# Forgetting attention and two feed-forward layers on one core: the first pair's scores without placement, and every other matmul on the whole array

## The chip, the core and the metric

One core of a Trainium2 chip runs the whole program. The metric is the device time of one execution in microseconds (us), from the first to the last instruction with what lies around it; lower is better. A core has five engines with queues of their own: TensorE (PE, with its weight loads as PEld), VectorE (DVE), ScalarE (ACT), GpSimd (POOL) and SyncE (SP), which here sends nearly all transfers. The transfers are carried out by 16 DMA engines.

## What is computed

An attention with 4 batches, 8 heads, 576 positions and 64 numbers per head, whose scores get a decay from a running sum of logarithms, and then two feed-forward layers on 2304 tokens of 512 numbers:

```python
scores = scale * np.matmul(q, k.transpose(0, 1, 3, 2))
log_f = np.log(np.clip(f, 0.0001, 1.0))
cum = np.cumsum(log_f, axis=-1)
decay = cum[:, :, :, None] - cum[:, :, None, :]
scores = np.where(causal, -1000000000.0, scores + decay)
attn = np.exp(scores - np.max(scores, axis=-1, keepdims=True))
attn = attn / (np.sum(attn, axis=-1, keepdims=True) + 1e-09)
x = np.matmul(attn, v)            # then laid out as 2304 x 512
h = x @ w_in;  x = (h - np.tanh(h)) @ w_out
h = x @ w_in2; out = (h / (1.0 + np.exp(-h))) @ w_out2
```

## The kernel before

**Precision.** Most matmuls run on numbers marked F32R, and the kernel splits each number into a rounded part hi and a rest lo and multiplies hi·hi, hi·lo and lo·hi. A matmul on plain float32 shows in the trace as two weight loads and two matmuls. The odd head's values (L548, L549) are of that second kind.

**Tiles.** Attention runs over 16 pairs of heads. A pair has nine tiles: four row blocks of 128 queries of the even head (i = 0 to 3, with 128 to 512 keys), a tile with the last 64 queries of both heads together (`h` = 2, `i` = 4), and four of the odd head. Tile n passes through `scores` two steps ahead, `least` (DVE, mask and minimum), `expo` (ACT, exponential and row sum), `guard` and `normalise` (DVE adds 1e-9 and takes the reciprocal of two tiles' sums, POOL multiplies), and after LAG = 9 steps `transposes` (PE), `evac_a` and `evac_b` (ACT, DVE) and `values` (PE). The order is written out by hand in the loop at L682; each engine works through its own queue in that order.

**Scores.** A score tile takes two matmuls. For them q and k, hi and lo, and the decay rows are placed by DMA (`place`, L394) into `kqa` (128 rows: hi over lo) and `kqb` (68 rows: the third product over four decay rows). There are two such buffers, for even and odd pairs. A pair's placement is ten transfers between places in SBUF and one of decay rows from DRAM, all on SP's queue. `split` (L378) makes hi and lo from the loaded `kqraw`, on POOL and DVE (in pair 0 also ACT). Pair 1's hi and lo lie in `pth` and `ptl`, which hold the transposed probabilities later; all others lie in one pair of buffers `kqhi`, `kqlo`.

**Decay rows.** `decay_rows` (L87) fills constants on POOL, clips f and scans its logarithm, and DVE and ACT write four rows per head into pair 1's still unused `kqa` and `kqb`. Two transfers take them to DRAM, from where each pair's placement reads its own.

**Values.** For the even head, `values` (L539) multiplies `vals` (hi and lo of v side by side, 128 columns) by `pth` and `ptl`. For the odd head it uses the 64 columns of `vraw` of that head and plain float32. Keys 512 to 575 are chunk c = 4, with 64 rows. The transposes of that chunk (L518) have 64 columns. `collect_a` and `collect_b` copy the outcome into x, and the odd head's goes from partitions 0 to 63 to 64 to 127.

**Feed-forward.** `hidden` (L252) and `project` (L311) run matmuls of 512 columns from the end of the attention on; `wload` and `wdecode` load and decode the weights, of which the first four chunks are loaded during the attention.

Of the kernel before, what the change touches and what calls it, by code (L numbers as in the profile page):

```python
# [7 lines left out]
F32 = mybir.dt.float32  # L8
# [18 lines left out]
NPT = 448 * 4 + S  # L27

# [9 lines left out]
def forgetting_attention_two_ffn(  # L38
# [25 lines left out]
    def setup_consts(const):  # L64
        ident = const.tile([P, P], F32, name="ident")
        nc.gpsimd.memset(ident, 0.0)
        nc.gpsimd.affine_select(
            out=ident, in_=ident, pattern=[[-1, P]], compare_op=ALU.not_equal,
            fill=1.0, base=0, channel_multiplier=1,
        )  # L70
# [5 lines left out]
        )  # L76
        mask4 = const.tile([P, S // 2], F32, name="mask4")
# [7 lines left out]
        return ident, mask, mask4  # L85

    def decay_rows(pool, ft, room):  # L87


        BH = B * H  # L90
        rows = [a[:, j, :] for a in room for j in range(2)]
        kc, q0, q1 = slice(K0, Q0), slice(Q0, Z1), slice(Q1, W)
        for r, a in enumerate(rows):
            nc.gpsimd.memset(rd(a[:, Z1:Q1]), 0.0)
            nc.gpsimd.memset(rd(a[:, 0:K0]), 0.0)
            for c in ((kc,) if r % 2 else (q0, q1)):
                nc.gpsimd.memset(rd(a[:, c]), 1.0 / SCALE)
        ones = pool.tile([P, S], F32, tag="p", name="ones")[0:BH]
        nc.vector.memset(ones, 1.0)
        nc.vector.tensor_scalar(ft, ft, 1e-4, 1.0, ALU.max, ALU.min)  # L100
        lf = pool.tile([P, S], F32, tag="p", name="lf")[0:BH]
        nc.scalar.activation(lf, ft, AF.Ln)
        cum = pool.tile([P, S], F32, tag="p", name="cum")[0:BH]
        nc.vector.tensor_tensor_scan(cum, ones, lf, 0.0, ALU.mult, ALU.add)
        nc.scalar.mul(rows[0][:, kc], cum, -1.0)
        nc.vector.tensor_copy(rows[1][:, q0], cum[:, 0:512])
        nc.vector.tensor_copy(rows[1][:, q1], cum[:, 512:S])
        nc.vector.tensor_tensor(rows[3][:, q0], cum[:, 0:512], rd(rows[1][:, q0]), ALU.subtract)
        nc.vector.tensor_tensor(rows[3][:, q1], cum[:, 512:S], rd(rows[1][:, q1]), ALU.subtract)
        nc.vector.scalar_tensor_tensor(  # L110
            rows[2][:, kc], cum, -1.0, rd(rows[0][:, kc]), ALU.mult, ALU.subtract
        )
        dec = dram.tile([4, BH, W], F32, name="dec")
        for i, a in enumerate(room):
            nc.sync.dma_start(out=dec[2 * i:2 * i + 2].rearrange("r p w -> p r w"), in_=rd(a))
        return dec
# [639 lines left out]
```

## Time and profile before

| | us |
|---|---|
| median of three runs | 1046.52 |
| lowest, highest | 1042.13, 1047.77 |
| the profiled execution | 1043.61 |
| its span, first to last instruction | 1041.5 |
| PE busy in it | 1001.6 (96%) |
| DVE, ACT, POOL busy | 612.3, 491.3, 199.8 |

The busy times are sums over stages with different limits: POOL works in the attention alone. In the traces, L12 is line 12 of the kernel, `out_t<-ptf,vraw 128*64 128x512` names the tile written and those read, the rows and columns of the array that the weights take, and the shape of what streams through. "x2" stands for two equal instructions one behind the other, given with the first one's start and the time from there to the last one's end.

### The profile page before, as it was taken

Reading aid. Unit: us, or ns where it says so; the run is one execution under the profiler, and the core shown is the slowest. Engines: PE = TensorE matmul, PEld = TensorE weight load, DVE = VectorE, ACT = ScalarE, POOL = GpSimd, SP = SyncE. Lnnn points to the kernel's source line nnn. Section 1 sums busy time; section 2 is a strip of 40 time slices with the busy share of each in tenths; the row PEclk is TensorE's granted clock in tenths of the full one; section 3 lists DMA queues with packets and bytes.
Section 4 is the critical chain, followed back from the end, with each engine's and each line's share of the span. In section 5 each row is a group of like instructions: output and inputs, shape, how many; then the busy total and the mean of one; then the engine's idle time right before and its main releaser. Section 6 shows DMA issues by size and latency. Waiting matters only on the chain.

```text
span 1041.5 us, 14028 instructions
## 1 busy us (share of the span) xinstructions
PE 1001.6 (96%) x4912; PEld 812.2 (78%) x4912; DVE 612.3 (59%) x1430; ACT 491.3 (47%) x1089; POOL 199.8 (19%) x293
## 2 busy tenths in 40 slices
PE   2599999999999999999999999999999999999998
PEld 2467666665888888898888988888888888888887
DVE  4479888988766646565556875334443555533323
ACT  3477778786545443343333543433443444332322
POOL 6578878887100000000000000000000000000000
PEclk9899999999999999999999999999999999999999
DMA  8988898742221201111102211101001111001111
GB/s 217 270 224 224 233 233 229 202 124 81 81 69 54 81 1 41 41 41 41 41 2 80 81 42 41 36 6 61 25 38 41 41 41 41 1 0 41 41 41 61
DMA packets 29621, 85.65 MB, mean 82 GB/s; under 512 B 4496, under 2 KB 4496, under 8 KB 29488
## 3 DMA queue, kind: packets, MB, share of 16 engines
q1 hardware_dynamic: 29552, 84.76, 28.1%
q8 instruction: 39, 0.64, 0.3%
q14 instruction: 30, 0.25, 0.1%
HBM read 49.49 MB, written 5.37 MB: 53 GB/s over the span
## 4 chain that ended last, share of the span: by engine, by line
PE 90%; DMA 4%; SPq 2%; DVE 2%; POOL 1%; issue 1%; ACT 1%; DVEq 0%; POOLq 0%
PE a L311 38%; PE h L252 38%; PE out_t L553 6%; PE t L507 4%; SPq L373 2%; DMA kqb<-kqhi 2%; PE s L431 1%; PE s L430 1%; DMA kqa<-pth 1%; PE misc L443 1%; PE s L443 1%; DMA kqa<-kqhi 1%; PE misc L553 1%; DMA kqa<-ptl 0%; DMA kqa<-kqlo 0%
## 5 line engine op out<-in xcount | busy, mean ns | idle before, releaser
L252 PE MATMUL h<-xh,wh 128*128 128x512 f32 (+1 forms) x640 | 236.3, 369 | 0.0
L252 PE MATMUL h<-xl,wh 128*128 128x512 f32 (+1 forms) x640 | 235.6, 368 | 0.0
L252 PE MATMUL h<-xh,wl 128*128 128x512 f32 (+1 forms) x640 | 235.4, 368 | 0.0
L274 DVE TENSOR_TENSOR gl<-g,gh 128x512 fp32r<-128x512 f32 (+1 forms) x158 | 101.4, 642 | 101.7 <-ACT gh L270 99.8
L252 PEld LDWEIGHTS h<-xh,wh 128*128 128x128 f32 x640 | 120.7, 189 | 23.3 <-issue 2.8
L270 ACT CAST gh<-g 128x512 fp32r<-128x512 f32 (+1 forms) x160 | 92.6, 579 | 95.0 <-DVE g L267 92.5
L252 PEld LDWEIGHTS h<-xl,wh 128*128 128x128 f32 x640 | 120.7, 189 | 20.2
L252 PEld LDWEIGHTS h<-xh,wl 128*128 128x128 f32 x640 | 120.5, 188 | 20.0
L311 PE MATMUL a<-gh,wh 128*128 128x512 f32 (+1 forms) x320 | 117.9, 368 | 0.0
L311 PE MATMUL a<-gl,wh 128*128 128x512 f32 (+1 forms) x320 | 117.8, 368 | 0.0
L311 PE MATMUL a<-gh,wl 128*128 128x512 f32 (+1 forms) x320 | 117.7, 368 | 0.0
L311 PE MATMUL a<-wh,gh 128*128 128x512 f32 x288 | 112.2, 390 | 0.0
L311 PE MATMUL a<-wl,gh 128*128 128x512 f32 x288 | 112.2, 390 | 0.0
L311 PE MATMUL a<-wh,gl 128*128 128x512 f32 x288 | 112.0, 389 | 0.0
L269 ACT ACTIVATE g<-h 128x512 f32<-128x512 f32 (+1 forms) x80 | 44.3, 554 | 113.6 <-PE h L252 98.5
L479 ACT ACTIVATE p<-p,mn 128x128 f32<-128x128 f32 (+2 forms) x144 | 84.8, 589 | 25.3 <-DVE mn L461 18.7
L240 DVE TENSOR_TENSOR xl<-y,xh 128x512 fp32r<-128x512 f32 (+1 forms) x60 | 37.4, 638 | 96.6 <-ACT xh L238 96.6
L493 POOL TENSOR_SCALAR p<-p,sm 128x128 f32<-128x128 f32 (+2 forms) x144 | 83.0, 590 | 40.8 <-DVE sm L490 30.2
L238 ACT CAST xh<-y 128x512 fp32r<-128x512 f32 (+1 forms) x60 | 34.2, 580 | 104.8 <-PE h L252 103.1
L507 PE MATMUL t<-ident,p 128*128 128x128 f32 x384 | 70.1, 285 | 12.0 <-DVE sm L486 7.3
L461 DVE CUSTOM_DVE_ANT_0 p<-s,mask 128x128 f32<-128x128 f32 (+2 forms) x144 | 68.2, 473 | 13.2 <-PE s L431 12.2
L507 PEld LDWEIGHTS t<-ident,p 128*128 128x128 f32 x384 | 48.4, 143 | 32.1 <-POOL kqhi L386 10.4
(110 smaller groups left out, 1625.6 us busy)
## 6 DMA issues: line engine op xcount, KB each, us to landing
raw<-w_in SPq DMA_DIRECT2D x32, 512.0 KB, 4.2
raw<-w_out SPq DMA_DIRECT2D x32, 512.0 KB, 4.1
kqraw<-kq SPq DMA_DIRECT2D x16, 608.0 KB, 7.1
kqa<-kqhi SPq DMA_DIRECT2D x30, 304.0 KB, 3.8
vraw<-v SPq DMA_DIRECT2D x16, 320.0 KB, 3.7
kqa<-kqhi SPq DMA_DIRECT2D x30, 160.0 KB, 3.8
kqb<-kqlo SPq DMA_DIRECT2D x30, 160.0 KB, 3.0
out<-ob SPq DMA_DIRECT2D x18, 256.0 KB, 2.0
```

The lines of the kernel that those rows point to most:

```text
L238: nc.scalar.copy(hi[:, :n], src[:, k, t0:t0 + n])
L240: eng.tensor_tensor(lo[:, :n], src[:, k, t0:t0 + n], rd(hi[:, :n]), ALU.subtract)
L252: nc.tensor.matmul(hp[:, :n], w[:, k * P:k * P + P], m[:, :n], start=(k == 0 and r == 0), stop=(k == NKT - 1 and r == 2),)
L269: nc.scalar.activation(g[:, :n], hp[:, :n], AF.Silu)
L270: nc.scalar.copy(gh[:, :n], g[:, :n])
L274: eng.tensor_tensor(gl[:, :n], g[:, :n], rd(gh[:, :n]), ALU.subtract)
L311: nc.tensor.matmul(dst, w, m, start=(first and r == 0), stop=(last and r == 2))
L461: nc.vector.tensor_tensor_reduce(out=pt[:, c0:c0 + src.shape[1]], in0=src, in1=m, op0=ALU.add, op1=ALU.min, scale=-SCALE, scalar=init, acc ...
L479: nc.scalar.activation(pt[:, :w], pt[:, :w], AF.Exp, bias=mn, scale=-1.0, accum_out=rowsum[n // 2][:, n % 2:n % 2 + 1],)
L493: nc.gpsimd.tensor_scalar(pt[:, :w], pt[:, :w], sm[:, j:j + 1], 1.0, ALU.mult, ALU.mult)
L507: nc.tensor.transpose(tp[:, c, :], pt[:, c * P:c * P + P], ident)
L553: nc.tensor.matmul(dst[0:m], w, pt[:ks, 448 * c + a:448 * c + q1], start=(c == 0 and r == 0), stop=(c == last and r == len(terms) - 1),)
```

## The change

Pair 0 is no longer placed. Its hi and lo lie in `pth` and `ptl`, and each score tile is made by four matmuls that read them where they are: hi·hi, hi·lo, lo·hi and one of decay rows, each on the 64 partitions of its head (partitions 0 to 63 or 64 to 127). The decay rows lie for it in `kqa` of pair 0, at partitions 0 and 64 of a zeroed tile. For its tail tile, both heads' last queries are copied into `last_q`, three 128 x 128 matrices with zeros elsewhere, so that four matmuls on all 128 rows serve both heads. Pair 1's hi and lo move to `kqhi` and `kqlo`.

All other matmuls take all rows and columns: the odd head's values take 128 columns of `vraw` (the 64 ahead of them are not used afterwards), chunk 4 takes 128 rows, its transpose takes 128 columns of tiles `pt4` whose last 64 columns are zeroed once. The odd head's outcome then lies on partitions 64 to 127 already.

`guard` and `normalise` handle three tiles at a time, every third step, and the guard adds a tile `eps` in place of a number. The decay rows are built in the memory of x and sent in one transfer; four short ones bring pair 0's back. The clip of f, the splits and the constants are put in another order, pair 0's low parts are all made on POOL and its hi on ACT, and the loads of pairs 2 and 3 and of v come behind pair 1's placement.

```diff
-            sp = pool(actx, "sp", LAG + 2)
+            sp = pool(actx, "sp", LAG + 1)
...
+            pt4 = [sp.tile([P, 640], F32, name=f"pt4_{i}", bufs=1) for i in range(2)]
...
+            first = (pth[:, 0:RAW], ptl[:, 0:RAW], kqt[0][0][:, 0, K0:W])
+            last_q = [ptl[:, RAW + 128 * j:RAW + 128 * j + 128] for j in range(3)]
...
-                    eng = nc.vector if p == 0 and j > 3 else nc.gpsimd
-                    eng.tensor_tensor(lo[:, c0:c1], raw[p][:, c0:c1], rd(hi[:, c0:c1]), ALU.subtract)
+                    sub(lo[:, c0:c1], raw[p][:, c0:c1], rd(hi[:, c0:c1]))
...
+            def first_dec():
+                for h in range(2):
+                    r = slice(64 * h, 64 * h + 4)
+                    nc.sync.dma_start(out=rd(first[2][r]), in_=dec[h])
+                    nc.sync.dma_start(out=rd(last_q[2][r, 64 * h:64 * h + 64]), in_=dec[h, :, TAIL])
...
+                if p == 0:
+                    hi, lo, de = (a[64 * h:64 * h + 64] for a in first)
+                    q = slice(S + P * i, S + P * i + P)
+                    for r, (a, b) in enumerate(((hi, hi), (hi, lo), (lo, hi), (de, de))):
+                        nc.tensor.matmul(s[:, :n], a[:, q], b[:, 0:n], start=r == 0, stop=r == 3)
+                    return
...
+                if p == 0:
+                    (hi, lo, de), (th, tl, td) = first, last_q
+                    for r, (a, b) in enumerate(((th, hi), (th, lo), (tl, hi), (td, de))):
+                        nc.tensor.matmul(dst, a, b[:, c0:c1], start=r == 0, stop=r == 3)
+                    return
...
             def guard(n):
-                sm = rowsum[n // 2]
-                nc.vector.tensor_scalar(sm, sm, 1e-9, None, ALU.add)
+                sm = rowsum[n // 3]
+                nc.vector.tensor_tensor(sm, sm, eps, ALU.add)
...
-                for j in range(2):
+                for j in range(3):
...
-                    t5, o = tp[0:64, 1, :], 448 * 4 + 512
-                    nc.tensor.transpose(t5, ptile.pop((p, 2, 4))[0][:, 512:S], ident)
+                    t5, o = tp[:, 1, :], 448 * 4 + 512
+                    nc.tensor.transpose(t5, ptile.pop((p, 2, 4))[0][:, 512:640], ident)
...
-                    ks = P if c < 4 else 64
                     if h == 0:
-                        w = vals[p][:ks, c].rearrange("p a d -> p (a d)")
+                        w = vals[p][:, c].rearrange("p a d -> p (a d)")
                         terms = (pth, ptl)
                     else:
-                        w = vraw[p][:ks, 1, D * c:D * c + D]
+                        w = vraw[p].rearrange("p h d -> p (h d)")[:, D * (c + 4):D * (c + 6)]
...
-                            dst[0:m], w, pt[:ks, 448 * c + a:448 * c + q1],
+                            dst, w, pt[:, 448 * c + a:448 * c + q1],
...
-                    nc.scalar.copy(x[64:128, hp, t0 + c0:t0 + c1], src[0:64])
+                    nc.scalar.copy(x[64:128, hp, t0 + c0:t0 + c1], src[64:128])
...
+            nc.vector.memset(scratch[0], 1.0)
+            nc.vector.memset(rd(first[2]), 0.0)
+            nc.vector.memset(rd(ptl[:, RAW:RAW + 384]), 0.0)
+            decay_consts(rows)
+            decay_rows(rows, scratch, ft, [(split, 0, 0), (split, 0, 1)])
+            mask, eps = setup_mask(const)
+            split_last(0)
+            for j in range(2, 6):
+                split(0, j)
+            split_last(1)
+            dec = dram.tile([BH, 4, RAW], F32, name="dec")
+            nc.sync.dma_start(out=dec, in_=rows)
+            first_dec()
+            for t in kqt[1] + kqt[0]:
+                nc.gpsimd.memset(rd(t[:, :, 0:K0]), 0.0)
+            for j in range(6):
+                split(1, j)
+            for h in range(2):
+                place(1, 0, [h])
+                place(1, 1, [h])
+                if h == 0:
+                    place(1, 2)
+            load_kq(2)
+            load_v(1)
             prep_v(0)
+            for a in pt4:
+                nc.gpsimd.memset(a[:, S:640], 0.0)
+            mask4, ident = setup_later(const)
...
-                if n % 2 == 0 and has(n - 4):
-                    guard(n - 4)
+                if n % 3 == 2 and has(n - 5):
+                    guard(n - 5)
```

## Rows read from the trace of the kernel before

**Rows 1.** The page: the chain that ended last, by line.

```profile
PE a L311 38%; PE h L252 38%; PE out_t L553 6%; PE t L507 4%; SPq L373 2%; DMA kqb<-kqhi 2%; PE s L431 1%; PE s L430 1%; DMA kqa<-pth 1%; PE misc L443 1%; PE s L443 1%; DMA kqa<-kqhi 1%; PE misc L553 1%; DMA kqa<-ptl 0%; DMA kqa<-kqlo 0%
```

**Rows 2.** Windows, start: length, PE, PEld, DVE, ACT, POOL busy, clock, DMA share, GB/s.

```profile
15.00:32.00 17.00, 8.79 (x27) 6.65 (x27) 6.66 (x27) 6.11 (x18) 7.65 (x12) 1.00 0.97 222
32.00:64.00 32.00, 23.82 (x120) 18.48 (x120) 18.01 (x75) 17.28 (x54) 14.59 (x23) 0.84 0.98 260
```

**Rows 3.** Windows of three pairs' periods: one of them, and the sum and mean.

```profile
89.15:101.88 12.73, 12.69 (x76) 8.86 (x75) 11.95 (x44) 10.00 (x32) 9.78 (x15) 1.00 0.88 226
...
sum 38.18, PE 38.06 PEld 26.56 DVE 34.20 ACT 30.48 POOL 31.72; mean PE 12.69 PEld 8.85 DVE 11.40 ACT 10.16 POOL 10.57
```

**Rows 4.** Timeline of PE (start, us, instruction): first scores of pairs 3, 4, 15.

```profile
63.69 0.31 PE L430 MATMUL s<-kqa 128*128 128x128 f32 x1
...
76.43 0.31 PE L430 MATMUL s<-kqa 128*128 128x128 f32 x1
...
219.40 0.31 PE L430 MATMUL s<-kqa 128*128 128x128 f32 x1
```

**Rows 5.** Timeline of PE inside one period, 91 to 101 us.

```profile
91.61 0.28 PE L553 MATMUL out_t<-ptl,vhl 128*128 128x192 f32 x1
...
92.23 0.42 PE L430 MATMUL s<-kqa 128*128 128x384 f32 x1
...
93.55 0.52 PE L507 MATMUL t<-ident,p 128*128 128x128 f32 x3
...
94.16 0.59 PE L553 MATMUL out_t<-ptf,vraw 128*64 128x512 f32 x1
...
94.59 0.59 PE L553 MATMUL out_t<-ptf,vraw 128*64 128x512 f32 x1
...
95.35 0.30 PE L443 MATMUL s<-kqb 68*128 68x288 f32 x1
...
95.76 0.60 PE L507 MATMUL t<-ident,p 128*128 128x128 f32 x4
...
96.26 0.28 PE L431 MATMUL s<-kqb 68*128 68x128 f32 x1
...
97.60 0.30 PE L443 MATMUL misc<-kqb 68*128 68x288 f32 x1
...
98.56 0.28 PE L431 MATMUL s<-kqb 68*128 68x256 f32 x1
...
99.90 0.34 PE L431 MATMUL s<-kqb 68*128 68x384 f32 x1
...
100.89 0.33 PE L507 MATMUL t<-ident,p 128*128 128x128 f32 x1
```

**Rows 6.** DVE's guards: groups by line, 89.15 to 114.6 us; timelines near 209 us.

```profile
L486 DVE TENSOR_SCALAR sm<-sm 128x2 f32<-128x2 f32 x9 | 3.3, 370 | 0.0
...
208.82 1.42 POOL L493 TENSOR_SCALAR p<-p,sm 128x512 f32<-128x512 f32 x2
...
209.62 0.65 DVE L486 TENSOR_SCALAR sm<-sm 128x2 f32<-128x2 f32 x1
```

**Rows 7.** Timeline of SP's sends (SPq) and DVE in the start.

```profile
0.74 0.40 SPq L583 DMA_DIRECT2D ft<-f  x1
...
2.70 0.45 DVE L100 TENSOR_SCALAR ft<-ft 32x576 f32<-32x576 f32 x1 [1.25 <-DMA ft<-f]
...
7.89 0.32 SPq L115 DMA_DIRECT2D dec<-kqb  x1
...
19.58 1.11 SPq L373 DMA_DIRECT2D kqa<-pth  x2
...
25.19 0.98 DVE L388 CAST kqhi<-kqraw 128x640 fp32r<-128x640 f32 x1 [1.91 <-DMA kqb<-dec]
...
46.70 0.49 DVE L388 CAST kqhi<-kqraw 128x640 fp32r<-128x640 f32 x1 [5.77 <-DMA kqb<-kqhi]
```

**Rows 8.** The chain that ended last, in order of time, near the attention's end.

```profile
246.90 1.52 DVE wa L154
```

## What the change does to the time, predicted before it ran

> **What bounds the kernel now.** I read the chain of work that ended last first, then the busy time by stage, then TensorE's instructions one by one inside one attention pair, and last the engines beside it. The page gives 76% of the chain to PE at the feed-forward lines L311 and L252, and 6 and 4% to the attention's values and transposes [rows 1]. The change touches neither of the first two, so what can move is the attention, a quarter of the profiled 1041.5 us. It has two stages. Up to about 62 us the DMA engines are the limit: they are 97 to 98% busy, while PE works 8.8 us of 17 and 23.8 us of 32 [rows 2]. After that PE is: 12.69 us busy in a period of 12.73 us [rows 3], and every pair starts its first score 12.74 us behind the last. The first score of pair 3 starts at 63.69 us and that of pair 15 at 219.40 us: 12 periods in 155.7 us, so 2.8 us of stalls beside 12 x 12.74 us [rows 4].
>
> **TensorE in one period: what whole-array matmuls remove.** In [rows 5] I compare starts, not durations, because matmuls overlap. Undisturbed, five instructions with 128 columns start 0.50 us apart in all (95.76 to 96.26), so I take 0.11 us each, also for shorter ones; a pass of an odd head over 512 columns takes 0.43 us (94.16 to 94.59), so 448, 320 and 192 columns take 0.38, 0.27 and 0.16, and a single-pass matmul half of that (288 columns 0.12, 384 columns 0.17). Wherever the array goes from whole to 64 columns or 64 rows or back, the starts are further apart:
> - even head, last 64 keys: from 91.61 to 92.23 four short ones start, 0.62 us against 4 x 0.11 = 0.44: 0.18 too much;
> - odd head, first part: 93.55 to 95.35, 1.80 us against three transposes 0.33, two short passes 0.22, two passes 0.86 and one score 0.12, 1.53 in all: 0.27;
> - 448 columns: 96.26 to 97.60, 1.34 us against 0.11 + 2 x 0.38 + 0.12 = 0.99: 0.35;
> - 320 columns: 98.56 to 99.90, 1.34 us against 0.12 + 2 x 0.27 + 2 x 0.11 + 0.17 = 1.05: 0.29;
> - 192 and 64 columns: 99.90 to 100.89, 0.99 us against 0.17 + 2 x 0.16 + 2 x 0.11 = 0.71: 0.28.
>
> The sum is 1.37 us; starts that the profile models a little late may be 0.1 of it, so I take 1.3 us per pair. After the change none of these matmuls uses a part of the array: odd heads load 128 columns, chunk 4 has 128 rows, the fifth transpose (L518) is whole. The price of the wider loads is already in it, since I count short ones at 0.11. PE alone would then need 12.73 - 1.3 = 11.4 us per pair.
>
> A page of the Trainium skill, TensorEngine Tiling (Array Packing), section Key Properties, says that changing the tiling mode, not just the tile, drains the engine. By that rule all of the 1.3 us goes; the trace agrees in so far as the gaps stand at each change of shape, [rows 5].
>
> **What is late next.** In the same three periods DVE is busy 11.40 us on average, POOL 10.57, ACT 10.16, the DMA engines 0.88 of one [rows 3]. DMA at 0.88 x 12.73 = 11.2 us is just under the new PE time. DVE loses guards and reciprocals: now 4.5 of each per pair, then 3. A guard takes 0.37 us on average [rows 6], a reciprocal I put at 0.15: 1.5 x 0.52 = 0.8 us off, so 10.6 us. The guard is long because it waits: the one that starts at 209.62 ends at 210.27, as the POOL work that began at 208.82 does at 210.24 [rows 6]. The new guard is a tensor_tensor with sums and eps both in SBUF. I price it as the old one, 0.37; with no wait (taken as a reciprocal, 0.15) DVE would lose another 0.7 us.
>
> The Trainium skill, SBUF — State Buffer, section SBUF: two separate sides, says the port pair shared with GpSimd is locked by a DVE instruction with two SBUF inputs as well as by one in a two-port mode. By it the new form still waits; by the hope that it doesn't DVE would come to 9.9 us. No run shows it yet.
>
> Normalising three tiles at once comes later for the oldest of them (four steps ahead of its transpose in place of five), and POOL gets its work in lumps. Four steps of a pair of nine last over 5 us, three normalisations about 2 us (0.65 each, POOL's 9.78 us over the 15 instructions of a period [rows 3]), so I cost this at nothing; if POOL is in the middle of a split, PE's transposes wait up to 1 us, which is in the bound. With four engines between 10.6 and 11.4 us, held together by queues in order, a period at exactly the PE sum is unlikely. I take 11.7 us: 1.03 us less than now; bounds 11.4 (PE alone) and 12.2 (DVE's busiest period, 11.95 us [rows 3], less 0.8, plus the 1 us by which periods now exceed DVE's work). Over 12 periods: 12.4 us, between 6 and 16. The 2.8 us of stalls stay.
>
> **The start.** Removed: pair 0's ten placement transfers, with its decay rows 1.91 MB by the shapes in the code. At 222 GB/s [rows 2] they are 8.6 us of a stage that DMA bounds. Added: a wait. SP now sends the decay rows to DRAM, must wait till they have landed before it sends four short reads of them, and behind these on SP's queue stand pair 1's placement and the loads of pair 2. Before the sends, DVE gets two fills more ahead of the clip at 2.70, 1600 elements a row; at the clip's own rate (576 in 0.45 us) they are 1.3 us, in an idle time of 1.25 us [rows 7]. I put the clip 0.2 us later, and the sending of the decay rows at 8.1 us in place of 7.89. Landing: f is sent at 0.74 and used at 2.70, 2.0 us for a small one [rows 7], plus 0.62 MB at 222 GB/s, 2.8 us: 12.9 us. Four sends at 0.55 us (two took 1.11 [rows 7]): 15.1 us, where pair 1's placement starts now at 19.58. Of the seven us from 8.1 to 15.1 the DMA engines work three, so 8.6 - 4 = 4.6 us of DMA time are gained net. A second look: pair 2's keys now follow pair 1's placement, 15.1 + 8.6 + 0.62 MB at 222 GB/s (2.8) = 26.5 us, while DVE splits them now at 25.19 [rows 7]. So the first step is a microsecond later, not earlier. But pair 1's scores no longer wait for a late placement, and pair 2's placement, which ends at 46.70 when DVE goes on with pair 3 [rows 7], has those 4.6 us of transfers less ahead of it: some 42 us. I take 5 us for the start; bounds 2 (the split at 26 us sets it) and 8.6 (all of the removed bytes).
>
> Pair 0's scores are four matmuls a tile on 64 rows in place of two: 16 more, in a stretch in which PE is half idle [rows 2], so nothing. Moving all of pair 0's low parts to POOL adds two of its instructions there, 1.3 us by the same 0.65, before the decay rows have landed: nothing. Building ident and mask4 later takes them out of the way; if it delayed the first transpose, some 1 us would show. The pair buffers and the p tiles hold as many tiles as before: nothing.
>
> **The end.** Behind pair 15's first score two pairs' values are still to come, 2 x 1.3 = 2.6 us of PE. But there the chain leaves PE: at 246.90 us it runs over DVE's weight decoding [rows 8]. I take half, 1.3 us (0 to 2.6).
>
> **How the numbers follow.** 5 + 12.4 + 1.3 = 18.7 us. Against the profiled execution's own 1043.61 us (its span and 2.1 us around it) that is 1024.9. The three other runs are 1042.13 to 1047.77 with a median 2.9 us higher; the mean of all four is 1045.0, and 1045.0 - 18.7 is 1026.
>
> **Rivals.**
> - *Another engine takes over at once.* DVE (with POOL holding its guards) or DMA allows 12.2 us. For it: DVE 11.95 of 12.73 us in one period [rows 3]. Against: it loses 0.8 us of work. 5 + 12 x 0.5 + 0.7 = 11.7 us: 1033. Chance 0.17.
> - *The gaps are not due to the shape.* Odd heads also change from one-pass to two-pass matmuls, and that stays. Then only the even head's 0.18 and some 0.1 around the 64 x 64 go: period 12.4, 5 + 3.6 + 0.4 = 9 us: 1036. Against it: the even head has no two-pass matmuls and shows the same gap when rows fall to 64 [rows 5]. Chance 0.10.
> - *Slower: wide two-pass matmuls cost more.* No row shows one with 128 columns of weights. An odd head's passes are 2 x 1600 columns per pair, 2.7 us. If the wide form took double, a period would be 12.73 - 1.3 + 2.7 = 14.1; 12 x 1.4 + 2.8 - 5 = 14.6 us slower: 1060. It decides from 1.7 us more per pair on (63% dearer), where 13 x 0.4 eats the start's 5. Against: one-pass matmuls with 64 and 128 rows or columns stream at the same rate. Chance 0.06.
> - *The start loses more than it gives* (the decay rows' round trip over 6 us late), steady gain kept: about 1031 to 1036, inside the range; chance 0.05.
>
> The forecast keeps 0.62. The range of 1017 to 1038 takes in the sum of the low bounds (8.6 + 16 + 2.6 = 27 us) and the first two rivals. Within 0.5% (5.2 us, about what a measurement of this kernel can tell from no change) would need most of the steady gain to vanish and little at the start: 0.06. Slower 0.06, faster 0.88.
>
> **What would show it.** Right: starts 0.11 us apart around every odd head's matmuls and the 64-key ones; first scores of neighbouring pairs 11.4 to 12 us apart from pair 3 on; pair 3's first score near 58 us; the feed-forward lines unchanged. Wrong: a two-pass 512 taking more than 0.43 us; gaps that stay at the type change; PE idle before scores, released by DVE, POOL or placements; DVE's split of pair 3 later than 44 us.

## The result, and the profile after

The changed kernel takes 1028.07 us (median of 4 runs, 1027.44 to 1028.68), the kernel before 1046.28 (4 runs beside them, 1042.13 to 1047.77): ratio 0.9832, 95% interval 0.9803 to 0.9861. Forecast were 1026 us and a range of 1017 to 1038. The profiled execution took 1028.68 us with a span of 1026.5, that of before 1043.61 with 1041.5, so 15.0 us of span are to be found. (The medians lie 18.2 us apart: the kernel before was profiled in an execution 2.7 us under its median, the changed one in one 0.6 us above. No trace shows where the other 3.2 us lie.) Where the 15.0 us lie is read from four marks: the first score of pair 3 (p3), that of pair 15 (p15), the first matmul of the last feed-forward sum (L315, before L311), and the end.

Timeline of PE after (start, us, instruction): first scores of pairs 3, 4 and 15, and the feed-forward's first 'a'; in the second fence its answer in the kernel before, whose first scores are in [rows 4].

```profile
59.65 0.31 PE L462 MATMUL s<-kqa 128*128 128x128 f32 x1
...
71.34 0.31 PE L462 MATMUL s<-kqa 128*128 128x128 f32 x1
...
205.62 0.31 PE L462 MATMUL s<-kqa 128*128 128x128 f32 x1
...
242.49 0.48 PE L315 MATMUL a<-gh,wh 128*128 128x512 f32 x1
```

```profile
257.69 0.50 PE L311 MATMUL a<-gh,wh 128*128 128x512 f32 x1
```

| stretch | before | after | gained | forecast |
|---|---|---|---|---|
| start, up to p3 | 63.69 | 59.65 | 4.0 | 5 |
| p3 to p15, 12 periods | 155.71 | 145.97 | 9.7 | 12.4 |
| p15 to the feed-forward | 38.29 | 36.87 | 1.4 | 1.3 |
| feed-forward to the end | 783.8 | 784.0 | -0.2 | 0 |

Inside a period, timeline of PE after, first the end of an even head with its last 64 keys, then an odd head's first two parts. They answer [rows 5]; the third fence has the lines of the kernel before that these rows leave out.

```profile
97.52 0.25 PE L588 MATMUL out_t<-pth,vhl 128*128 128x192 f32 x1
97.61 0.27 PE L588 MATMUL out_t<-ptl,vhl 128*128 128x192 f32 x1
...
97.89 0.33 PE L543 MATMUL t<-ident,p 128*128 128x128 f32 x1
```

```profile
87.96 1.08 PE L588 MATMUL out_t<-ptf,vraw 128*128 128x512 f32 x2
...
89.00 0.30 PE L479 MATMUL s<-kqb 68*128 68x288 f32 x1
...
89.91 0.28 PE L463 MATMUL s<-kqb 68*128 68x128 f32 x1
90.02 0.97 PE L588 MATMUL out_t<-ptf,vraw 128*128 128x448 f32 x2
...
90.95 0.29 PE L479 MATMUL misc<-kqb 68*128 68x288 f32 x1
```

```profile
91.52 0.25 PE L553 MATMUL out_t<-pth,vhl 128*128 128x192 f32 x1
...
92.15 0.33 PE L507 MATMUL t<-ident,p 128*128 128x128 f32 x1
...
96.46 0.96 PE L553 MATMUL out_t<-ptf,vraw 128*64 128x448 f32 x2
```

The two matmuls of 192 columns and the two of 64 at the even head's end take 0.37 us from the first start to the transpose behind them (97.52 to 97.89) where they took 0.63 (91.52 to 92.15). A change from one-pass to two-pass work shows no gap: the score at 89.91 is followed after 0.11 us. Nor does the one shape that is still not whole, the scores' second matmul with its 68 rows, as before: this same score is one of them. From two passes of 448 columns to the second score behind them (90.02 to 90.95) it is 0.93 us, against 1.13 before (96.46 to 97.60).

Busy time by stretch after (length, then PE, PEld, DVE, ACT, POOL busy with their counts, granted clock, DMA share, GB/s): the start, then the periods of pairs 4, 5 and 6, for [rows 2, 3].

```profile
15.00:32.00 17.00, 11.24 (x35) 9.14 (x36) 5.15 (x22) 4.37 (x14) 4.29 (x12) 1.00 0.85 230
32.00:64.00 32.00, 27.68 (x148) 22.84 (x148) 21.96 (x86) 21.57 (x67) 23.98 (x37) 0.95 0.96 253
71.34:82.92 11.58, 11.44 (x76) 9.57 (x75) 10.89 (x41) 10.53 (x34) 9.77 (x16) 1.00 0.93 247
82.92:95.14 12.22, 11.76 (x76) 9.62 (x75) 11.88 (x42) 10.63 (x35) 10.15 (x16) 1.00 0.93 244
95.14:107.19 12.05, 11.64 (x76) 9.62 (x75) 10.92 (x40) 9.74 (x30) 11.44 (x17) 1.00 0.91 236
```

The shortest period of this profile is 11.58 us long, and PE is busy for 11.44 of it: PE still sets it, but DVE, ACT and POOL now stand within 2 us of it and the DMA engines at 0.93, and the next two periods already have 0.5 to 0.6 us of stalls. Two of these small stalls, in the timelines of PE and DVE: in the first PE waits since the cast ahead, at 92.58, took 0.82 us beside POOL's L393; in the second, 0.82 us of PE at 180.82, the cast had waited for a placement.

```profile
94.13 0.41 PE L543 MATMUL t<-ident,p 128*128 128x128 f32 x2 [0.32 <-DVE sm L522]
```

```profile
179.58 0.49 DVE L396 CAST kqhi<-kqraw 128x640 fp32r<-128x640 f32 x1 [0.91 <-DMA kqa<-kqhi]
```

**The largest stall**, timelines after of PE, DVE and POOL near 118 us, and the window behind it:

```profile
119.55 0.41 PE L543 MATMUL t<-ident,p 128*128 128x128 f32 x2 [1.75 <-DVE sm L522]
```

```profile
115.98 2.83 DVE L396 CAST kqhi<-kqraw 128x640 fp32r<-128x640 f32 x1
```

```profile
114.88 1.70 POOL L529 TENSOR_SCALAR p<-p,sm 128x256 f32<-128x256 f32 x3
116.56 1.27 POOL L181 TENSOR_TENSOR wl<-wl,wb 128x512 fp32r<-128x512 f32 x1
117.80 0.66 POOL L393 TENSOR_SCALAR kqhi<-kqraw 128x576 fp32r<-128x576 f32 x1
```

```profile
121.00:124.50 3.50, 3.50 (x14) 3.12 (x14) 2.52 (x11) 1.04 (x5) 3.50 (x5) 0.51 0.96 318
```

DVE's cast of pair 9's high parts (0.49 us by the median of its 15) lasts 2.83 us: it ends at 118.81, 0.34 us behind the end of POOL's L393 (118.47), about as long as a cast takes alone. PE's transposes wait 1.75 us behind it, and from 121.0 to 124.5 PE runs at 0.51, its 1.2 GHz level, which costs another 1.75 us. Together 3.5 us: the period p7 to p8 is 13.38 us and p8 to p9 13.33, against 11.58.

### The profile page after: what moved, and what is told of

The parts are those of the page before. It is cut to its first block, busy times and chain, and to the rows that moved or that the text cites. A ratio compares the mean times of both kernels' runs of the same rounds, so it can differ in the third digit from the quotient of the medians.

```text
span 1026.5 us, 13933 instructions
## 1 busy us (share of the span) xinstructions
PE 990.1 (96%) x4928; PEld 828.3 (81%) x4928; DVE 608.5 (59%) x1382; ACT 492.5 (48%) x1092; POOL 200.2 (19%) x288
## 4 chain that ended last, share of the span: by engine, by line
PE 88%; DVE 4%; DMA 4%; ACT 2%; SPq 2%; issue 1%; POOL 0%; DVEq 0%; ACTq 0%; POOLq 0%
PE a L315 38%; PE h L256 38%; PE out_t L588 4%; PE t L543 3%; SPq L381 1%; PE s L462 1%; PE s L463 1%; DMA kqb<-kqhi 1%; DMA kqa<-kqhi 1%; DVE kqhi L396 1%; PE s L479 1%; DVE ptl L570 1%; DMA kqraw<-kq 1%; PE misc L479 0%; ACT p L515 0%
## 5 line engine op out<-in xcount | busy, mean ns | idle before, releaser
L315 PE MATMUL a<-gh,wh 128*128 128x512 f32 (+1 forms) x320 | 117.9, 369 | 0.0
L315 PE MATMUL a<-gl,wh 128*128 128x512 f32 (+1 forms) x320 | 117.8, 368 | 0.0
L315 PE MATMUL a<-gh,wl 128*128 128x512 f32 (+1 forms) x320 | 117.7, 368 | 0.0
L315 PE MATMUL a<-wh,gh 128*128 128x512 f32 x288 | 112.2, 390 | 0.0
L315 PE MATMUL a<-wl,gh 128*128 128x512 f32 x288 | 112.2, 390 | 0.0
L315 PE MATMUL a<-wh,gl 128*128 128x512 f32 x288 | 112.0, 389 | 0.0
L515 ACT ACTIVATE p<-p,mn 128x128 f32<-128x128 f32 (+3 forms) x128 | 72.2, 565 | 24.7 <-DVE mn L497 20.5
L529 POOL TENSOR_SCALAR p<-p,sm 128x128 f32<-128x128 f32 (+3 forms) x128 | 70.6, 565 | 19.4 <-DVE sm L526 14.8
L244 DVE TENSOR_TENSOR xl<-x,xh 128x512 fp32r<-128x512 f32 (+1 forms) x56 | 34.5, 634 | 62.3 <-ACT xh L242 62.3
L543 PE MATMUL t<-ident,p 128*128 128x128 f32 x320 | 59.6, 286 | 9.6 <-DVE sm L522 6.6
L315 PEld LDWEIGHTS a<-gh,wh 128*128 128x128 f32 x320 | 60.3, 189 | 10.4 <-ACT x L599 0.4
```

Of the source, the lines that this page charges most:

```text
L244: eng.tensor_tensor(lo[:, :n], src[:, k, t0:t0 + n], rd(hi[:, :n]), ALU.subtract)
L315: nc.tensor.matmul(dst, w, m, start=(first and r == 0), stop=(last and r == 2))
L515: nc.scalar.activation(pt[:, :w], pt[:, :w], AF.Exp, bias=mn, scale=-1.0, accum_out=rowsum[n // 3][:, n % 3:n % 3 + 1],)
L529: nc.gpsimd.tensor_scalar(pt[:, :w], pt[:, :w], sm[:, j:j + 1], 1.0, ALU.mult, ALU.mult)
L543: nc.tensor.transpose(tp[:, c, :], pt[:, c * P:c * P + P], ident)
```

## The experiments

All are the changed kernel with one edit, but for the second (the kernel before with a part of the change) and the last (three edits). Each was timed in 3 rounds (the last in 5) beside the kernel before; ratios are against it, and the brackets behind a ratio hold its 95% interval. That of the changed kernel, 0.9803 to 0.9861, overlaps those of all kernels below but the first two, so small differences are read from profiles, of which each kernel has one.

### Is it the whole array? The change without it, and it alone

Theory: the whole array gives the steady gain and the end, the rest of the change the start. Rival: the gain comes from the guards or from the placements left out.

```
-  w = vraw[p] ... [:, D*(c+4):D*(c+6)];  matmul(dst, w, pt[:, ...])       # odd head
+  w = vraw[p][:ks, 1, D*c:D*c+D];  matmul(dst[0:m], w, pt[:ks, ...])      # ks = 64 in chunk 4
   (and the fifth transpose and its copies back to 64 rows, the odd head's outcome back to partitions 0 to 63)
```

> The changed kernel with one part undone: odd heads' values on 64 columns, chunk 4 on 64 rows, its transpose on 64 columns, as before. Theory (the gaps at changes of shape are PE's time): gaps of 0.1 us are back around these matmuls, first scores of neighbouring pairs 12.7 us apart when nothing stalls, about 12.95 on average; start unchanged (pair 3's first score near 59.7 us). 12 x 0.8 + 1.3 = 11 us more than the changed kernel: 1039 us, 1037 to 1041. Rival (the start and the guards for three tiles carry the gain, the array's shape does not): 1028 to 1031 us.

1040.37 us (1039.09 to 1040.43), ratio 0.9944 (0.9926 to 0.9962). Timeline of PE: first scores of p3 and p15.

```profile
57.55 0.31 PE L462 MATMUL s<-kqa 128*128 128x128 f32 x1
...
216.04 0.31 PE L462 MATMUL s<-kqa 128*128 128x128 f32 x1
```

Without the whole array p3 to p15 takes 158.49 us, in the changed kernel 145.97: 12.5 us. From p15 to the feed-forward it is 38.34 against 36.87: 1.5 us. The undisturbed period is 12.75, where it was 12.73 to 12.74 before.

The second kernel is the one before with the same lines of the whole array and nothing else (the fifth tile gets its own two buffers of 640 columns, and to make room the decay's scratch rows lie in the memory of x).

> The kernel before with the whole-array matmuls alone (odd heads 128 columns, chunk 4 128 rows); pair 0 is placed and guards take two tiles as before. Theory: the periods shorten as in the changed kernel, 11.6 us when nothing stalls, start as before (pair 3 near 63.7 us): 1046.3 - 11 = 1035 us, 1033 to 1038; the upper end if guards for two tiles cost DVE some 0.2 us per period. Rival (shape is not the cause): 1046 us.

1035.37 us (1034.9 to 1036.99), ratio 0.9902 (0.9883 to 0.992). p3 stays at 62.78 us and p15 comes at 210.99: 148.21 us for the 12 periods, 7.5 us less than before. The two parts, 0.0056 and 0.0098, add up to 0.0154 of the whole change's 0.0168: both are real, and the whole array is the larger. The end is not the whole array's alone, though: in this kernel's profile the time from p15 to the end of the span is 822.7 us, in the kernel before 822.1, without the whole array 822.2, and only in the changed kernel 820.8. Here and in the next kernel, both with guards for two tiles, PE waits 1.9 us for DVE some 27.5 us behind p15, and a stretch at 0.5 of the clock follows, which the changed kernel's end does not have.

### The guards

Two questions: whether a guard waits for POOL whatever its form, and whether DVE's work on guards makes the stalls. Three kernels: guards for two tiles as a tensor_scalar, no guard, and the guard for three as a tensor_scalar.

```
-  if n % 3 == 2 and has(n - 5): guard(n - 5)          # and normalise
+  if n % 2 == 0 and has(n - 4): guard(n - 4)
```

> The changed kernel with guards and normalisation for two tiles, and the guard a tensor_scalar, as before. Theory (DVE, waiting for POOL, makes the stalls between pair 3 and 15, 6.8 us of them in the changed kernel's trace): 0.8 us more DVE work per period, a mean period of 12.3 to 12.6 us in place of 12.16: 1030 to 1033 us. Rival (DVE has room, the stalls come from the placements): 1028 us, no difference.

1032.23 us (1027.81 to 1034.93), ratio 0.9865 (0.9834 to 0.9896). The interval overlaps that of the changed kernel, so the three tiles are worth between nothing and some 4 us: not settled. The profile, of the fastest of its runs (1027.81), does not bear out the way of the theory: p3 to p15 takes 146.12 us, a mean period of 12.18 and not 12.3 to 12.6; only behind p15 it takes 1.9 us more than the changed kernel.

```
-  nc.vector.tensor_tensor(sm, sm, eps, ALU.add)
+  pass
```

> The changed kernel without the guard: the addition of 1e-9 to the row sums is left out. Theory (DVE): 1.2 us less DVE work per period and no guard that waits for POOL; undisturbed periods stay at 11.6 us because PE sets them, the 6.8 us of stalls fall to 3 or 4: 1024 to 1026 us. Rival (stalls come from the placements or the weights' loads): 1028 us.

1024.61 us (1022.86 to 1026.47), ratio 0.9795 (0.977 to 0.982). The time is the theory's, the way is not. In its profile p3 is 2.3 us earlier, which is the start's doing (rows sent at 8.25 us, see below), and p3 to p15 takes 145.10 us, only 0.9 less: of the 6.8 us of stalls 5.9 are left, where 3 to 4 were expected. Windows from 60 to 200 us, the changed kernel and this one:

```profile
60.00:200.00 140.00, 134.58 (x840) 111.39 (x840) 125.28 (x462) 118.25 (x363) 121.12 (x179) 0.99 0.91 238
```

```profile
60.00:200.00 140.00, 133.37 (x852) 111.11 (x852) 116.00 (x425) 119.15 (x366) 121.27 (x180) 1.00 0.91 239
```

DVE has 9.3 us less to do, 0.8 per period, and the periods hardly shorten: DVE's sum is not what makes the stalls.

```
-  nc.vector.tensor_tensor(sm, sm, eps, ALU.add)
+  nc.vector.tensor_scalar(sm, sm, 1e-9, None, ALU.add)
```

> The changed kernel with the guard for three tiles as a tensor_scalar with the number 1e-9 in place of a tensor_tensor with eps in SBUF. Theory (what the guard waits for is the SBUF port that it shares with POOL, and a tensor_tensor with two SBUF inputs needs it): guards of three numbers as tensor_scalar take 0.15 to 0.2 us if they don't use the second port, then 1025 us, near the kernel without guard; if they wait like the old ones of two numbers (mean 0.37), 1028 us. Rival (the guard waits for its input, not for a port): durations as in the changed kernel, mean 0.42, and 1028 us.

1028.41 us (1026.62 to 1031.66): no difference. All guards in one line (min/median/max in ns), first of the changed kernel, then of this one, then the reciprocals of the changed kernel:

```profile
L522 DVE TENSOR_TENSOR sm<-sm,eps x48: 144/356/1261, 30.3 to 224.3; 128x3 f32<-128x3 f32 x48
```

```profile
L522 DVE TENSOR_SCALAR sm<-sm x48: 152/433/1278, 30.8 to 223.9; 128x3 f32<-128x3 f32 x48
```

```profile
L526 DVE RECIPROCAL sm<-sm x48: 163/165/175, 31.0 to 224.5; 128x3 f32<-128x3 f32 x48
```

An addition to three numbers waits in either form, as its predecessor for two did [rows 6]; a reciprocal of the same three never does.

### The start

Theory: pair 2's keys stand behind the wait for the decay rows on SP's queue, and DVE needs them (4.44 us idle, below). The edit moves two loads ahead of it:

```
   nc.sync.dma_start(out=dec, in_=rows)
+  load_kq(2)
+  load_v(1)
   first_dec()
   ...                       # placement of pair 1
-  load_kq(2)
-  load_v(1)
```

> The changed kernel with the loads of pair 2's q and k and pair 1's v sent behind the decay rows, ahead of SP's wait for them, instead of behind pair 1's placement. Theory (in the start DVE stands 4.4 us before it can split pair 2, till its keys land at 29.8 us, while the DMA engines idled from 12 to 16 us): DVE splits pair 2 near 25.5 us, when pair 1's placement has been read; pair 3's first score 3 to 4 us earlier, 56 us: 1024.5 us, 1023.5 to 1026. Rival (the bytes of the placements set the start whatever the order): 1027 to 1028 us.

1025.42 us (1024.04 to 1026.49), ratio 0.9808 (0.9774 to 0.9842). Timeline of DVE, the cast of pair 2's high parts (at 25.19 us before, [rows 7]), in the changed kernel, here, and in the kernel with the late weights (below), whose start is the changed kernel's:

```profile
29.84 0.49 DVE L396 CAST kqhi<-kqraw 128x640 fp32r<-128x640 f32 x1 [4.44 <-DMA kqraw<-kq]
```

```profile
24.76 0.49 DVE L396 CAST kqhi<-kqraw 128x640 fp32r<-128x640 f32 x1
```

```profile
28.30 0.49 DVE L396 CAST kqhi<-kqraw 128x640 fp32r<-128x640 f32 x1 [5.00 <-DMA kqraw<-kq]
```

It comes 5.1 us earlier, p3 at 56.39 us, 3.3 us earlier; p15 is 4.4 us earlier. But not all of it is the edit's: here the decay rows were sent at 8.28 us, in the changed kernel's profile at 10.25. Among the kernels that send near 8.25 and keep the old order the cast stands at 27.7 to 28.5 and p3 at 57.2 to 58.3 us. Against these the early loads win 3.0 to 3.7 us at the cast and 0.8 to 1.9 at p3, and 1.1 us of the 4.4 at p15 lie behind p3, where the low clock after PE's wait of 1.76 us is missing.

The second question of the start is why the decay rows were sent at 10.25 us and not at 8.1. The timelines of the changed kernel's SP, DVE and POOL:

```profile
10.25 0.33 SPq L636 DMA_DIRECT2D dec<-x  x1
```

```profile
5.97 0.80 DVE L117 CAST x<-x 32x64 fp32r<-32x64 f32 x1
6.69 1.32 DVE L118 TENSOR_TENSOR x<-x 32x512 fp32r<-32x512 f32 x1
7.94 0.87 DVE L119 TENSOR_TENSOR x<-x 32x64 fp32r<-32x64 f32 x1
8.74 1.42 DVE L120 SCALAR_TENSOR_TENSOR x<-x 32x576 fp32r<-32x576 f32 x1
```

```profile
5.92 3.63 POOL L384 TENSOR_TENSOR ptl<-kqraw,pth 128x288 fp32r<-128x288 f32 x4 [1.49 <-ACT pth L396]
```

DVE makes the rows while POOL makes pair 0's low parts. The next kernel moves these to DVE, behind the rows:

```
-  sub(lo[:, c0:c1], ...)
+  (nc.gpsimd if p else nc.vector).tensor_tensor(lo[:, c0:c1], ..., ALU.subtract)
```

> The changed kernel with one edit: the low parts of the first pair are made on DVE, behind the decay rows, and not on GpSimd beside them. Theory: the decay rows were sent at 10.25 and not at 8.1 us since DVE's copies and differences of the rows (0.80, 1.32, 0.87 and 1.42 us, against 0.27, 0.67, 0.20 and 0.78 before) ran beside GpSimd's four subtractions. With these gone from GpSimd the rows are sent near 8.2, the placements of the second pair begin near 14, p3's first score stands near 58 and not 59.65, and the time is 1025.5 to 1027. Rival: the start is set by the loads that stand on SP's queue behind the rows, and DVE's own low parts delay the first pair's scores as much; the time is 1027.5 to 1029.

1026.72 us (1025.06 to 1028.22), ratio 0.9828 (0.9803 to 0.9853): within the noise of the changed kernel. The rows are now sent at 7.96 us, L118 and L120 take 0.68 and 0.75, and p3 is at 57.78; but pair 8's first score, at 120.58, is where it was (120.57). So the rows go early where POOL does not work beside DVE. The 1.9 us show at p3, but they were lost again in between, as in a stall of 1.42 us at 81.61, where DVE had waited 1.47 us for a placement (kqb<-kqhi).

The kernels that leave this part alone tell more, and this edit alone would not show the cause. Of the eleven profiles with pair 0's low parts on POOL, eight have the rows sent at 8.23 to 8.28 us, one at 9.57, and two (the changed kernel and the tensor_scalar for three) at 10.25 and 10.27. The kernel with the late weights (below) has the same start:

```profile
8.23 0.33 SPq L636 DMA_DIRECT2D dec<-x  x1
```

```profile
5.89 4.79 POOL L384 TENSOR_TENSOR ptl<-kqraw,pth 128x288 fp32r<-128x288 f32 x4 [1.45 <-ACT pth L396]
```

Here POOL's four subtractions take 4.79 us and DVE's L118 to L120 0.67, 0.21 and 0.74; p3 is at 57.21. Which engine waits for which changes from one profile to the next, with the same instructions on both, and the profiled execution of the changed kernel was one in which DVE waited: some 2 us of its start are that. Each kernel has one profile, so no run shows whether it changes between executions of one kernel too.

### The middle: what the stalls are

Theory one: the DMA engines, where the placements and the second chunk's weights meet. Theory two: DVE, which waits for POOL. First, one placement transfer of five less per head from pair 3 on (the scores of those pairs are then made from older rows):

```
-  dma(ta[64:128, h, Q0:W], hi[s, S:RAW])
+  if p < 3:
+      dma(ta[64:128, h, Q0:W], hi[s, S:RAW])
```

> The changed kernel without one of the placement's transfers from pair 3 on: the second copy of q's high part into kqa is left out, 0.33 MB of 1.91 MB per pair, so those pairs' scores are computed from older rows. Theory (stalls come from DVE waiting for POOL): nearly nothing, 1027 us; the one stall that the profile puts down to placements, near 173 us, goes: 1026 to 1028 us. Rival (DMA, 91 to 94% busy, is what keeps the mean period at 12.16): 1022 to 1024 us.

1025.99 us (1024.62 to 1026.66), ratio 0.9813 (0.978 to 0.9845). The DMA share from 60 to 200 us falls from 0.91 to 0.83, p3 to p15 by 1.4 us only. Of that, 0.7 us is the period p12 to p13 (12.62 to 11.90), whose cast had waited for a placement; the stall of 1.75 us stays, here at 116.2. Transfers have a small part.

Next, the cast that is starved goes to ACT:

```
-  (nc.vector.tensor_copy if p else nc.scalar.copy)(hi[:, c], raw[p][:, c])
+  nc.scalar.copy(hi[:, c], raw[p][:, c])
```

> The changed kernel with q's high part made on ACT in place of DVE for every pair (640 numbers a row). Theory (DVE's copies between SBUF and SBUF wait for POOL, up to 2.8 us, and PE then stalls): DVE loses 0.5 to 2.8 us per pair, ACT gains 0.7 of 11.6 us: 1025 us, 1023 to 1027. Rival (ACT, at 10.3 us per period before, becomes the bound): 1028 to 1031 us.

1031.95 us (1030.74 to 1033.35), ratio 0.9876 (0.9836 to 0.9915): slower than the changed kernel by 4 us, so the expectation missed. The stall at 118 is gone; another, longer one stands 15 us later. Timelines of ACT and PE, and the chain of work in order of time:

```profile
133.00 0.73 ACT L396 CAST kqhi<-kqraw 128x640 fp32r<-128x640 f32 x1 [4.20 <-DMA kqb<-kqlo]
```

```profile
134.88 0.88 PE L543 MATMUL t<-ident,p 128*128 128x128 f32 x3 [4.54 <-DVE ptl L570]
```

```profile
124.19 8.72 DMA kqb<-kqhi
```

A placement transfer that otherwise lands in 3 to 5 us takes 8.72, behind the load of the second chunk's weights (1.05 MB), sent at 118.7 and 119.2 us (DMA share 0.99 from 120 to 133 us). The kernel without the whole array shows the same one (2.77 us at 135.99, behind a placement of 8.81 us), and the kernel before too, where the period of pair 8 is 14.92 us. In the changed kernel the starved cast comes first; that it hides this stall is argued, not shown, and no run has the cast on ACT and the weights late.

So the weights were loaded later:

```
-  if not stages[k]:
+  if not stages[k] and k > 0:
       wload(k + 2)
+  at(-10, wload, 2)
```

> The changed kernel with one edit: the second feed-forward chunk's weights (a load of about 1 MB) are fetched near the end of the pairs, and not in their middle, as soon as the first chunk's are decoded. Theory: the stalls that grew in the middle of the shortened pairs (from 2.8 to 6.8 us in all over p3 to p15) come from the placements and this load meeting on the DMA engines, as the wait of 'kqb<-kqlo' and 'kqb<-kqhi' near 120 to 133 us shows where the cast was moved to ACT. Then the periods p8 to p10 (13.4 and 13.3 us) fall to 11.6 to 12.3, and the time to 1024.5 to 1026. Rival: the stall belongs to DVE alone, which waits behind GpSimd's two-input work; then the 2.8 us cast near 116 us and PE's gap of 1.75 us near 118 stay, and the time is 1027.5 to 1029.

1025.35 us (1024.35 to 1026.18), ratio 0.9815 (0.9793 to 0.9837). The time is the theory's, the way is not: p3 to p15 takes 145.51 us, 0.5 less. The cast near 113 us still lasts 2.8 us and PE waits 1.73 behind it; only the low clock behind it is gone (p8 to p9 12.10 us), and small stalls took that place. Nor is that shown to be the weights' doing: with the early loads and with one placement less, whose weights come as in the changed kernel, no low clock follows the same wait either (1.76 and 1.75 us). The profile's gain is the start, where the rows went out at 8.23. The time alone would have confirmed a theory that its profile does not.

And POOL's weight decoding was moved to other steps, so that it does not stand where DVE casts:

```
-  at(9*(k//2+1) + (2, 6)[k % 2] - N, wdecode, ...)
+  at(9*(k//2+1) + (6, 9)[k % 2] - N, wdecode, ...)
```

> The changed kernel with one edit: the steps at which weights are decoded on GpSimd move from 2 and 6 to 6 and 9 of each nine, so that GpSimd's normalising, weight decoding and low-part subtraction don't stand back to back where DVE makes its cast of a pair's high parts. Theory: the cast of 2.8 us (median cast 0.49) is one DVE instruction starved by three GpSimd instructions in a row; with a gap between them it falls under 1.5 us, PE's gap of 1.75 us and the 3.4 us at the lower clock behind it go, and the time is 1024 to 1026. Rival: the load on GpSimd and DMA is the same and another stall takes the place of this one; the time is 1027 to 1029.5.

1027.4 us (1026.59 to 1032.25), ratio 0.9851 (0.9816 to 0.9885): the rival. The longest cast is now 1.07 us, but a guard takes the place of it. DVE, POOL, PE and the window behind:

```profile
117.54 3.73 DVE L522 TENSOR_TENSOR sm<-sm,eps 128x3 f32<-128x3 f32 x1
```

```profile
116.29 1.41 POOL L529 TENSOR_SCALAR p<-p,sm 128x128 f32<-128x128 f32 x3
117.64 1.58 POOL L384 TENSOR_TENSOR kqlo<-kqraw,kqhi 128x288 fp32r<-128x288 f32 x2
119.16 1.28 POOL L181 TENSOR_TENSOR wl<-wl,wb 128x512 fp32r<-128x512 f32 x1
120.38 0.87 POOL L384 TENSOR_TENSOR kqlo<-kqraw,kqhi 128x320 fp32r<-128x320 f32 x1
```

```profile
121.93 0.69 PE L462 MATMUL s<-kqa 128*128 128x384 f32 x1 [2.71 <-DVE mn L497]
```

```profile
121.50:128.00 6.50, 6.07 (x19) 4.51 (x20) 4.50 (x20) 3.77 (x13) 5.84 (x9) 0.52 0.72 170
```

An addition to three numbers, 0.14 us without a wait, took 3.73 us, until POOL's run of instructions ended; then PE ran at its lower level, 0.52 over the 6.5 us of the window. Moving the work moves the stall.

### Three together

Early loads, no guards, late weights in one kernel:

> The changed kernel with three edits put together: the keys of pair 2 and the values of pair 1 are loaded behind the decay rows' send, the 1e-9 isn't added to the sums of the tiles (it is the part of the computation that is left out; a sum is at least 1, so float32 does not show it), and the second chunk's weights are fetched late. Theory: the three act at different places (the start: p3's first score near 56.4 us and not 59.65; DVE's 48 small instructions; the DMA engines in the middle), but the pairs behind p3 keep a mean period near 12.1 us, since another starved DVE instruction or another load takes the place of each stall that goes, as the moved decode slots showed. So the gains come from the start, and p15's first score stands near 201 us: 1022 to 1024.5. Rival: each stall is a price of its own and the gains add (2.65 for the loads, 3.46 for the sums, 2.72 for the weights, from 1028.07): 1019 to 1021.

1024.19 us (1022.69 to 1027.37, 5 runs), ratio 0.9813 (0.9789 to 0.9837). The gains don't add. In its profile, the fastest of its runs, p3 is at 56.43 us and p3 to p15 takes 143.49, and the cast of 2.8 us is there still. Against the kernel with no guards alone (1024.61) nothing is gained that can be told.

## Why the prediction was right, and where its steps were off

**The whole array: right.** 1.3 us per pair were forecast from gaps between starts; measured are 12.74 - 11.58 = 1.16 us in the changed kernel's shortest period. The 0.2 us between this and PE's sum of 11.4 are small waits: the kernel with the moved decode slots has a period of 11.38 us with the same matmuls, and four others have one of 11.38 or 11.39. Its first scores of pairs 7 and 8:

```profile
104.78 0.31 PE L462 MATMUL s<-kqa 128*128 128x128 f32 x1
...
116.16 0.31 PE L462 MATMUL s<-kqa 128*128 128x128 f32 x1
```

So 12.73 - 11.38 = 1.35 us came back of the 1.37 read ahead; the five groups, 6.09 us before and 4.72 as I counted them for after, take 4.70 there. Within them the odd heads' passes cost a little more than counted: 512 columns with the score behind them take 1.04 us (87.96 to 89.00) where I counted 0.98, 448 columns 0.93 where I counted 0.88. The second pass of 512 starts 0.49 us behind the first, so one sign that I had named as wrong, over 0.43 us, did show, at a price of some 0.06; the even head's short ones make up for it. The rival of dear wide matmuls (1060 us) fell with that, and the one of the type change (1036) with the missing gaps there. The Trainium skill's TensorEngine Tiling (Array Packing), Key Properties, that a change of mode drains the engine, agrees with this: the gaps went where the shape no longer changes.

**The 12 periods: PE's sum right, the waits too cheap.** Forecast were 12 x 11.7 us and 2.8 us of stalls, 143.2 in all; it took 146.0, between that and the 149.7 (155.7 less 12 x 0.5) of the first rival, in which another engine takes over. Seven of the 12 periods are longer than the 11.4 to 12 us that I had named as a sign of being right. Above 12 x 11.4 I had allowed 3.6 us and 2.8 of stalls, 6.4 us in all; it was 9.2. The largest stall costs 3.5 us (p7 to p9), where the largest before cost 2.2 (a period of 14.92), and it is another one: before it was DVE's wait for a placement behind the weights' load, now it is a starved cast and the low clock. The rest are small waits for DVE, which POOL or a placement had held up: the first rival was there in part, but not as a new bound of 12.2 us. The step that failed is "The 2.8 us of stalls stay", with 0.3 us per period beside it: that was no price but a hope; with PE's slack gone each wait shows. DVE's price was off as well: I took 0.8 us off its period, and it went from 11.40 to 11.23 us on average (periods 4 to 6), since a guard takes 0.42 us and not 0.37 and the cast of the high parts, in these periods, 0.75 and not 0.55. But the 2.8 us by which 146.0 is over 143.2 do not come from there: without the guards DVE has the 0.8 us less that I had hoped for, and the 12 periods are 0.9 us shorter.

**The start: 5 forecast, 4.0 in this execution, 6 to 6.5 in most other profiles.** p3 was to be near 58 us; in eight of the nine kernels with the changed start and the rows sent before 8.3 us, early loads and low parts on DVE among them, it is at 56.4 to 57.8, and 58.3 in the other. The send at 8.1 us was right for these. The step that failed is "pair 0's low parts on POOL: nothing": in the profiled execution they held DVE's rows for 2 us. Pair 1's placement began at 15.98 (15.1 forecast), pair 2's cast at 29.84 (26.5). A second term was too low there: the load of pair 2's keys, sent behind the placement at 24.49, was used 5.35 us later, where I counted 2.8. So the cast is late (28.30) even where the rows went at 8.23 and the placement began at 13.96.

**The guards: right.** Neither form is spared the wait. By the Trainium skill's SBUF — State Buffer, section SBUF: two separate sides, the pair is locked for a whole instruction by whoever starts first. The trace agrees as far as one instruction goes; but the DVE cast that was due at 115.98 waited out not only the POOL instruction begun at 115.89 but the two behind it, and at 6.66 us, in the kernel with the late weights, POOL's subtraction let DVE's next three through (2.14 us for 0.79). Who comes next where both have a queue isn't in that rule and isn't settled here.

**The end: right in size**, 1.4 us against 1.3, but not by PE's work alone: it shows only with the whole array and guards for three tiles together (820.8 us behind p15, with either alone 822.2 to 822.7, before 822.1, in one profile each), and guards for three tiles were no part of that term. The feed-forward lines are unchanged.

**The sum.** The parts give 15.0 us in the profiled executions, where 18.7 were forecast; the medians lie 18.2 apart. So that 1028.07 came within 2.1 us of the 1026 forecast does not show that each part was right: where they could be measured they are 3.7 us short.

**What stays open:** whether the 3.5 us go if the cast or guard is kept off POOL and the weights are loaded late at once (each was tried alone); what three tiles a guard are worth; why the rows are sent 2 us later in some profiles; and why the clock falls behind one wait of 1.75 us and not behind another.

## What to carry to other kernels

Gaps between matmul starts wherever the array's shape changes are a price that can be read ahead and, in a period without waits, won back in full (here 1.35 us of 1.37); sum them over a period before anything is built. When the bound engine gives back its last slack, re-price every stall of the engines beside it, and look for places where DVE's short instructions meet a run of POOL's: that run, not their own length, is their price. Compare marks inside the profiles and not the times alone, since a confirmed time can have another cause, and look first whether the two profiles agree in the parts that the edit leaves alone.

## What was new about the hardware

- One DVE instruction can lose to several POOL instructions in a row: 2.83 us for a cast of 0.49, and 3.73 us for an addition to three numbers of 0.14. A reciprocal of the same size took 163 to 175 ns in all 48 cases.
- The same instructions on DVE and POOL, which begin within 0.1 us of each other, ended 2 us apart in the profiles of different kernels (rows sent at 8.23 or 10.25 us).
- After PE was idle 1.75 us, its clock was at the 1.2 GHz level (0.51) for 3.5 us; after 2.71 us idle, for 6.5 us (0.52). The length of the wait alone does not decide it: 1.73 us idle in the kernel with the late weights, 1.76 with the early loads and 2.14 in the kernel before had no such stretch behind them.
